# One fixed group for a unit's scores, another's sums and a third's transposes beside the first layer, and fewer pieces of w_out times phi

## The chip, the cores and the metric

The kernel runs on one NeuronCore of one Trainium2 chip. The metric is device time in microseconds (us): the median of several executions, beside one execution that the hardware profiler recorded.

## What is computed

The reference is a windowed attention followed by two mixture layers, in float32:

```python
# q, k, v: 4 batches x 8 heads x 576 positions x 64
scores = q @ k.T / 8                      # masked: a window of 32, or 32 dilated by 4
attn   = softmax(scores); x = attn @ v    # x becomes 2304 x 512
gate = sigmoid(x @ w_gate); val = x @ w_val      # 512 -> 1536
x    = (gate * val) @ w_out                      # 1536 -> 512
logits = x @ phi                                 # 32 slots
d = softmax over tokens(logits); slot_input = d.T @ x
slot_out = relu(slot_input @ w1[e]) @ w2[e]      # 8 experts, 4 slots each
out = softmax over slots(logits) @ slot_out
```

The kernel never forms x after `w_out`: it multiplies `w_out` by `phi` once (the tile `wp`) and takes the logits from the gated hidden values.

## The kernel before

**Token blocks and units.** Tokens are five blocks `n` (0 to 3 of 512 tokens, 4 of 256). A unit is one block and one pair of heads `hp`. Block 0's four units run at the start; the 16 units of blocks 1 to 4 are numbered z = 0 to 15 and run beside the first mixture layer. A unit has scores on PE (`scores`: one mask matmul and 32 small products, for each of two PSUM banks of the pool `ps_a`), a softmax on DVE, ACT and POOL (`softmax`, into `u["s"]`), four PE transposes (`turn_unit`, through a bank of `ps_m`, copied by ACT into a slot of `pt_ring`), the sums with v on PE (`weighted`, into the second halves of the score banks of a later unit, or for the last units into two banks of `ps_m`) and the copies into x, split into a high and a low part (`finish_unit`).

**The first layer.** `l1(n, f, ...)` computes feature block f (12 of them) of token block n: two halves (gate and value) of 12 matmuls of 512 columns into a bank of `ps_l1`. After each half it calls `between()`. Layer calls for block 0 and then block 1 give 48 such calls. A `Spread` object holds the list of unit steps and runs as many at a call as its marks make due. From the beginning of layer 0 on, the matmuls of the units go through `at()`, which pins an instruction behind everything traced before it on its engine; the layer's own matmuls and, before the change, the pieces of `w_out` times `phi` are not pinned, and the planner may place them earlier or later.

**The list of steps.** Unit z's scores, the sums of unit z - 2 and its copies are one step (`sp_step`), the transposes of unit z - 1 are another (`t_step`): 34 steps, 10 of them due by call 22, all by call 44.

**Weights.** `convert` takes staged 64-bit words (`st`, tag "l2", two buffers, 1 MB each) and makes float32 (`fw`), on ACT, DVE and POOL; the result is stored to DRAM at the next conversion. Conversions 12 to 17 are the six pieces of `w_out`, made during block 1's layer, one after each of its feature blocks 0 to 5; their `fw` use the tags "gb" and "xt" by turns ("xt" has one buffer). After each, `slot_weights` schedules four pieces for PE, each on a tick (a call of `between` during block 1): two of four transposes (`turned`), `product` and `summed`, beginning three ticks later.

**SP's queue.** All loads and stores up to the end of this layer are issued by SP in the order of the program: qk and v loads of units, staging loads, stores of converted weights, reloads of weights. The softmax of a unit of block 4 lives in the unused columns of its own qk buffer (two buffers), that of the other units in `sm4` (tag "x4").

After the first layer of blocks 0 and 1 come their logits and gathers (`Post`), blocks 2 and 3 as pairs (`pair_l1`), block 4, and the experts.

Of the kernel before, what the change touches and what calls it, by code (L numbers as in the profile page):

```python
# [7 lines left out]
F32 = mybir.dt.float32  # L8
# [9 lines left out]
P = 128  # L18
# [3 lines left out]
HP_ORDER = [0, 2, 1, 3]  # L22
NF = 12
# [6 lines left out]
SPL = (False, False)  # L30
NRM = True
C0 = 21
C1 = 19
WP = 1
ND = 4
# [21 lines left out]
def tile_kernel(  # L57
# [10 lines left out]
    nc = tc.nc  # L68

    cpool = ctx.enter_context(tc.tile_pool(name="cpool", bufs=1))  # L70
# [4 lines left out]
    ps_a = ctx.enter_context(tc.tile_pool(name="ps_a", bufs=4, space=PSUM))  # L75
# [1 line left out]

    BUFS = {
        "xa": 2, "xb": 2, "ga": 3, "gb": 3, "w": 2, "l2": 2,
        "qk": 2, "v": 2, "bd": 1, "xt": 1, "ws": 2, "x4": 1,  # L80
    }

    def b8(tag, shape, dt, name):
        return big.tile(shape, dt, tag=tag, name=name, bufs=BUFS[tag])
# [4 lines left out]
    ident = cst[:, 0 : C_I4 - C_ID]  # L89
    ones32 = cst[:, C_I4 - C_ID : C_PHI - C_ID]  # L90
    i4 = ones32[:, 0:32]
    phi = cst[:, C_PHI - C_ID : C_COLS - C_ID].rearrange("p (k s) -> p k s", k=ND)
    acc = cpool.tile([P, 3, 512], F32, name="acc")
# [43 lines left out]
    def at(ins):  # L137
        return tc.keep_in_program_order(ins) if grouped[0] else ins
# [52 lines left out]
    def turn_unit(u):  # L191
        s = u["s"].rearrange("p (c x) -> p c x", c=4)
        tr = ps_m.tile([P, 4, P], F32, tag="m", name="tr")
        for c in range(4):
            at(nc.tensor.transpose(tr[:, c], s[:, c], ident))  # L195
        nc.scalar.copy(pt_ring[:, u["z"] % 4].rearrange("p c i q -> p c (i q)"), tr)
# [53 lines left out]
            nc.scalar.copy(hi, xp[y])  # L250
            nc.vector.tensor_tensor(lo, xp[y], hi.bitcast(F32), ALU.subtract)  # L251

    sm4 = b8("x4", [P, 4, 512], F32, "sm4")
    early = [True]

    def ld(ins):
# [2 lines left out]
    def attn_steps(pbs, norm, head=None):  # L259
        jobs = [(n, hp) for n in pbs for hp in HP_ORDER]  # L260
        us = [{"id": j, "z": z} for z, j in enumerate(jobs)]
        tags = ["qk", "qk", "gb", "gb"] if head else ["qk"] * len(jobs)

        def load_qk(z):
            n, hp = jobs[z]
            w = 512 + k_cols(n, hp)
            us[z]["qk"] = b8(tags[z], [P, 2048], F32, "qk")
            us[z]["s"] = sm4[:, HP_ORDER.index(hp)] if n < 4 else us[z]["qk"][:, 1536:2048]
            ld(nc.sync.dma_start(us[z]["qk"][:, 0:w], qkv[n * NHP + hp, :, VCOLS : VCOLS + w]))

        def load_v(z):
            n, hp = jobs[z]
            if z % 2 == 0:
                v2 = b8("v", [P, 2, VCOLS], F32, "v2")
                us[z]["v"], us[z + 1]["v"] = v2[:, 0], v2[:, 1]
            ld(nc.sync.dma_start(us[z]["v"], qkv[n * NHP + hp, :, 0:VCOLS]))

        def load(z, what):
            if z < len(us) and not head:
                what(z)  # L280

        begun = []

        def first(what):
            if what not in begun:
                begun.append(what)
                what(0)
                what(1)

        def s_step(z, ts=range(4)):  # L290
            if z == 0 and 0 in ts:
                if head:
                    load_qk(0)
                    ld(nc.sync.dma_start(msk, masks.bitcast(BF16)))
                    load_qk(1)
                    ld(nc.sync.dma_start(cst, consts))
                    load_v(0)
                    load_qk(2)
                    load_v(1)
                    head()  # L300
                    load_qk(3)
                    load_v(2)
                    load_v(3)
                else:
                    first(load_qk)
                    first(load_v)
            scores(us[z], ts)
            if 3 not in ts:
                return
            if 2 <= z and not head:  # L310
                weighted(us[z - 2], range(2), us[z])
            softmax(us[z], norm)
            load(z + 2, load_qk)
            if z == 0:
                load(2, load_v)

        def t_step(z):
            turn_unit(us[z])

        def p_step(z, ts=range(2)):  # L320
            if head or z + 2 >= len(us):
                weighted(us[z], ts)
            if head:
                keep_warm(WP)
            if 1 in ts:
                finish_unit(us[z])
                load(z + 3, load_v)

        def sp_step(z):
            if z < len(jobs):  # L330
                s_step(z)
            if z >= 2:
                p_step(z - 2)

        steps = []
        for z in range(len(jobs) + (1 if head else 2)):
            turned = [(t_step, z - 1)] if 0 < z <= len(jobs) else []
            if head:
                score = [(s_step, z, [t]) for t in range(4)] if z < len(jobs) else []
                steps += score + turned + ([(p_step, z - 1, [t]) for t in range(2)] if z else [])  # L340
            else:
                steps += [(sp_step, z)] + turned
        return steps, lambda: first(load_qk), lambda: first(load_v)


# [21 lines left out]
    def convert(z):  # L367
        i = n_conv[0]
        n_conv[0] += 1
        stage(z)  # L370
        if i + 1 < len(turn):
            stage(turn[i + 1])
        st = staged[z]
        store()
        fw = b8(("ws", "ws", "gb", "xt")[i % 4] if i < NF else ("gb", "xt")[i % 2], [P, 2, 1024], F32, "fw")
        for h in range(2):
            c = slice(512 * h, 512 * h + 512)
            top, low = fw[:, 0, c], fw[:, 1, c]
            nc.scalar.activation(top, st[:, c, 1].bitcast(F32), AF.Prelu, scale=2.0**-112, alpha=2.0**32)  # L379
            nc.vector.tensor_scalar(top.bitcast(U32), top.bitcast(U32), 3, None, ALU.logical_shift_left)  # L380
            nc.vector.tensor_scalar(low.bitcast(I32), st[:, c, 0], 2.0**-29, None, ALU.mult)  # L381
            nc.gpsimd.tensor_tensor(low.bitcast(I32), top.bitcast(I32), low.bitcast(I32), ALU.add)  # L382
        if z < NF:
            stores.append((wg32[z // 2][:, z % 2], fw[:, 1]))
        else:
            y = z - NF
            stores.append((wo32[y // 2][:, 2 * (y % 2) : 2 * (y % 2) + 2].rearrange("p a c -> p (a c)"), fw[:, 1]))
            slot_weights(2 * y, fw[:, 1].rearrange("p (c x) -> p c x", c=2), 3)
        return fw[:, 1]

    ticks = [0]
    later = []
# [7 lines left out]
    def slot_weights(f, wo_f, lag):  # L400

        wt = pm.rearrange("p a b -> p (a b)").rearrange("p (k c x) -> p k c x", k=ND, c=2)
        at_ = {}

        def turned(c):
            wt_ps = ps_a.tile([P, ND, P], F32, tag="a", name="wt_ps")
            for kc in range(ND):
                nc.tensor.transpose(wt_ps[:, kc], wo_f[:, c, P * kc : P * kc + P], ident)
            nc.scalar.copy(wt[:, :, c], wt_ps)

        def product():
            pt_ps = ps_m.tile([P, 2, P], F32, tag="m", name="pt_ps")
            for kc in range(ND):
                nc.tensor.matmul(
                    pt_ps[32 * kc : 32 * kc + 32], lhsT=phi[:, kc, :], rhs=wt[:, kc], start=True, stop=True
                )
            at_["pt"] = cpool.tile([P, 2, P], F32, tag="pt", name="pt")
            nc.vector.tensor_copy(at_["pt"], pt_ps)

        def summed():  # L420
            wp_ps = ps_m.tile([P, 2, 32], F32, tag="m", name="wp_ps")
            for c in range(2):
                nc.tensor.matmul(wp_ps[:, c], lhsT=at_["pt"][:, c], rhs=i4, start=True, stop=True)
            nc.vector.tensor_scalar(wp[:, f : f + 2], wp_ps, 0.5, None, ALU.mult)

        for n, (step, *args) in enumerate(((turned, 0), (turned, 1), (product,), (summed,))):
            later.append((ticks[0] + lag + n, step, args))

    def split_w(src, pool=(True, False)):
        whl = b8("w", [P, 2, 2, ND, P], F32R, "whl")  # L430
# [454 lines left out]
    for z, (fn, *args) in enumerate(attn_steps([0], nc.vector, lambda: stage(0))[0]):  # L885
        fn(*args)
        if z == C0:
            steps, first_qk, first_v = attn_steps([1, 2, 3, 4], nc.gpsimd)
            sab = Spread(steps, [(2 * NF - 2, 10), (4 * NF - 4, len(steps))])
            ahead(0)  # L890
            first_qk()
            ahead(1)
            first_v()
# [128 lines left out]
    for f in range(NF):  # L1022
        c = f % 4
# [18 lines left out]
    for e in range(8):  # L1042
        for h in range(2):
            for kc in range(ND):
                nc.tensor.matmul(  # L1045
                    h_ps[h][32 * kc : 32 * kc + 32],
                    lhsT=st[:, kc, 32 * e : 32 * e + 32],
                    rhs=ew[0, e, h][:, kc],
# [230 lines left out]
```

## Time and profile before

| what | value |
|---|---|
| median of three runs | 498.02 us (497.69 to 499.08) |
| the profiled execution | 496.94 us |
| its span, first to last instruction | 495.2 us |
| PE busy | 468.6 us (95%) |
| DVE / ACT / POOL busy | 311.0 / 213.1 / 156.8 us |
| mean granted TensorE clock | 0.992 of full |

PE is TensorE's matmuls, PEld its weight loads, DVE VectorE, ACT ScalarE, POOL GpSimd, SP SyncE (here it only issues DMA). An `L` with a number is the line of the kernel that issued the instruction. The span is one execution; the median comes from others and also holds what lies around the span.

### The profile page before, as it was taken

Reading aid. Unit: us, or ns where it says so; the run is one execution under the profiler, and the core shown is the slowest. Engines: PE = TensorE matmul, PEld = TensorE weight load, DVE = VectorE, ACT = ScalarE, POOL = GpSimd, SP = SyncE. Lnnn points to the kernel's source line nnn. Section 1 sums busy time; section 2 is a strip of 40 time slices with the busy share of each in tenths; the row PEclk is TensorE's granted clock in tenths of the full one; section 3 lists DMA queues with packets and bytes.
Section 4 is the critical chain, followed back from the end, with each engine's and each line's share of the span. In section 5 each row is a group of like instructions: output and inputs, shape, how many; then the busy total and the mean of one; then the engine's idle time right before and its main releaser. Section 6 shows DMA issues by size and latency. Waiting matters only on the chain.

```text
span 495.2 us, 12830 instructions
## 1 busy us (share of the span) xinstructions
PE 468.6 (95%) x5488; PEld 357.3 (72%) x5488; DVE 311.0 (63%) x629; ACT 213.1 (43%) x414; POOL 156.8 (32%) x132
## 2 busy tenths in 40 slices
PE   6889999999899998999889999999999999999993
PEld 3558888887788876886557888888887889742552
DVE  3879898758666745436987656655547765541532
ACT  2455645435445534314744554554535343300223
POOL 0244536416445314235154323334212124110100
PEclk9899999999999999999999999999999999999998
DMA  8979978995896079120002201201499886579997
GB/s 301 421 276 361 351 234 306 310 344 195 322 368 253 2 253 394 63 86 1 1 1 86 85 25 61 86 5 80 142 372 422 345 326 259 190 296 367 428 402 239
DMA packets 23785, 112.14 MB, mean 226 GB/s; under 512 B 2352, under 2 KB 7216, under 8 KB 14640
## 3 DMA queue, kind: packets, MB, share of 16 engines
q1 hardware_dynamic: 23408, 111.06, 60.0%
q8 instruction: 43, 0.70, 0.6%
q10 hardware_dynamic: 320, 0.26, 0.2%
q14 instruction: 14, 0.11, 0.1%
HBM read 97.16 MB, written 14.16 MB: 225 GB/s over the span
## 4 chain that ended last, share of the span: by engine, by line
PE 80%; DVE 8%; DMA 4%; ACT 2%; issue 2%; POOL 1%; SPq 1%; DVEq 0%; ACTq 0%
PE l1ps L470 32%; PE pa L592 11%; PE pe L592 6%; PE tp L757 3%; PE s_ps L222 3%; PE h_ps L1045 3%; PE lt_ps L721 3%; PE pd L592 3%; PE s_ps L162 3%; PE so_ps L1104 3%; DMA wo<-fw 2%; PE sp L786 2%; PE tr L195 2%; DMA qk<-qkv 2%; DVE s L556 1%
## 5 line engine op out<-in xcount | busy, mean ns | idle before, releaser
L470 PE MATMUL l1ps<-x_hi,whl 128*128 128x512 f32 x384 | 129.4, 402 | 2.6 <-ACT x_hi L250 2.5
L470 PEld LDWEIGHTS l1ps<-x_hi,whl 128*128 128x128 f32 x384 | 71.7, 188 | 19.0 <-ACT x_hi L250 3.2
L470 PE MATMUL l1ps<-x_lo,whl 128*128 128x512 f32 x192 | 75.6, 394 | 0.0
L382 POOL TENSOR_TENSOR fw<-fw 128x512 int32<-128x512 int32 x36 | 49.0, 1370 | 61.7 <-DVE fw L381 24.7
L470 PEld LDWEIGHTS l1ps<-x_lo,whl 128*128 128x128 f32 x192 | 36.2, 188 | 6.6 <-DVE x_lo L251 0.2
L456 DVE SCALAR_TENSOR_TENSOR g<-g,l1ps 128x512 f32<-128x512 f32 (+1 forms) x36 | 21.4, 594 | 29.3 <-PE l1ps L470 29.0
L470 PE MATMUL l1ps<-x,whl 128*128 128x256 f32 x288 | 37.0, 285 | 0.0
L470 PEld LDWEIGHTS l1ps<-x,whl 128*128 128x128 f32 x288 | 35.4, 192 | 0.4 <-issue 0.2
L480 ACT ACTIVATE g<-l1ps 128x512 f32<-128x512 f32 (+1 forms) x36 | 18.9, 526 | 37.4 <-PE l1ps L470 37.4
L434 POOL TENSOR_TENSOR whl<-w,whl 128x512 fp32r<-128x512 f32 x12 | 15.9, 1326 | 51.2 <-ACT whl L433 39.7
L379 ACT ACTIVATE fw<-st 128x512 f32<-128x512 f32 x36 | 22.8, 675 | 12.4 <-DMA st<-wd 9.2
L757 PE MATMUL tp<-cst,g 128*128 128x128 f32 x216 | 28.0, 275 | 0.0
L757 PEld LDWEIGHTS tp<-cst,g 128*128 128x128 f32 x216 | 24.0, 140 | 5.0 <-issue 3.3
L762 ACT COPY gt<-tp 128x512 f32<-128x512 f32 x27 | 15.6, 584 | 25.0 <-PE tp L757 21.9
L176 DVE TENSOR_REDUCE mx<-s_ps 128x4 f32<-128x256 f32 x40 | 15.2, 413 | 14.3 <-PE s_ps L162 8.4
L380 DVE TENSOR_SCALAR fw<-fw 128x512 uint32<-128x512 uint32 x36 | 22.7, 640 | 1.9 <-ACT fw L379 1.0
L655 DVE TENSOR_TENSOR tm<-pe,tm 128x512 f32<-128x512 f32 x12 | 8.3, 691 | 24.1 <-PE pe L592 24.1
L434 DVE TENSOR_TENSOR whl<-fw,whl 128x512 fp32r<-128x512 f32 x24 | 20.9, 884 | 3.7 <-ACT whl L433 3.2
L381 DVE TENSOR_SCALAR fw<-st 128x512 int32<-128x512 uint32 x36 | 17.8, 528 | 7.7 <-DMA wst<-wg 3.7
L189 POOL TENSOR_TENSOR sm<-sm,su 128x512 f32<-128x512 f32 x12 | 13.6, 1130 | 28.3 <-DVE su L188 26.4
L434 POOL TENSOR_TENSOR whl<-wst,whl 128x512 fp32r<-128x512 f32 x12 | 15.9, 1326 | 19.0 <-ACT whl L433 11.7
L433 ACT CAST whl<-fw 128x512 fp32r<-128x512 f32 x24 | 14.6, 620 | 16.1 <-POOL fw L382 11.7
(455 smaller groups left out, 962.1 us busy)
## 6 DMA issues: line engine op xcount, KB each, us to landing
ew<-w SPq DMA_DIRECT2D x32, 1024.0 KB, 7.8
st<-wd SPq DMA_DIRECT2D x18, 1024.0 KB, 9.1
wst<-wg SPq DMA_DIRECT2D x12, 1024.0 KB, 7.7
v<-qkv SPq DMA_DIRECT2D x20, 512.0 KB, 6.1
wg<-fw SPq DMA_DIRECT2D x12, 512.0 KB, 7.8
w<-wg SPq DMA_DIRECT2D x6, 1024.0 KB, 7.5
qk<-qkv SPq DMA_DIRECT2D x10, 576.0 KB, 5.7
qk<-qkv SPq DMA_DIRECT2D x8, 528.0 KB, 5.5
```

The source lines that it names most:

```text
L176: nc.vector.tensor_reduce(mx[:, 4 * r : 4 * r + 4], u["s_ps"][r], AX.X, ALU.max)
L379: nc.scalar.activation(top, st[:, c, 1].bitcast(F32), AF.Prelu, scale=2.0**-112, alpha=2.0**32)
L380: nc.vector.tensor_scalar(top.bitcast(U32), top.bitcast(U32), 3, None, ALU.logical_shift_left)
L381: nc.vector.tensor_scalar(low.bitcast(I32), st[:, c, 0], 2.0**-29, None, ALU.mult)
L382: nc.gpsimd.tensor_tensor(low.bitcast(I32), top.bitcast(I32), low.bitcast(I32), ALU.add)
L434: (nc.gpsimd if pool[h] else nc.vector).tensor_tensor(whl[:, 1, h], src[:, h], whl[:, 0, h].bitcast(F32), ALU.subtract)
L456: return nc.vector.scalar_tensor_tensor(g, g, 1.0, val, ALU.add, ALU.mult)
L470: nc.tensor.matmul(pt[:, 0:nt], lhsT=whl[:, w_, a, dc, :], rhs=x_[n][:, dc, :], start=first, stop=(dc == HP_ORDER[-1] and w_ == 1),)
L480: nc.scalar.activation(g, pt[:, 0:nt], AF.Tanh, scale=0.5)
L592: nc.tensor.matmul(pt, lhsT=w[:, w_, P * c : P * c + P], rhs=x_[:, c], start=first and c == 0 and w_ == 0 and x_ is hi, stop=c == 1 and w_ ...
L757: nc.tensor.transpose(tp[:, c], g_sb[self.n, 4 * q + c][:, P * j : P * j + P], ident)
L762: nc.scalar.copy(to, tp)
```

## The change

Each group now holds, in program order: the scores of unit z, the sums of unit z - 3, the transposes of unit z - 2, the softmax of z, the loads, and the copies of unit z - 3. There are 19 steps, 7 due by call 22 and all by call 44. The softmax of block 4 gets a tile of tag "l2"; "xt" gets a second buffer. The pieces of `w_out` are three (both sets of transposes in one), pinned, and begin four ticks after a conversion, so that pieces of neighbouring conversions fall on the same ticks. The tile `pt` becomes a part of `acc`, and the descriptor scratch at the bottom of SBUF is set to 1024 bytes.

```diff
-        "qk": 2, "v": 2, "bd": 1, "xt": 1, "ws": 2, "x4": 1,
+        "qk": 2, "v": 2, "bd": 1, "xt": 2, "ws": 2, "x4": 1,
...
-            us[z]["s"] = sm4[:, HP_ORDER.index(hp)] if n < 4 else us[z]["qk"][:, 1536:2048]
+            if (n, hp) == (4, HP_ORDER[0]):
+                homes.append(b8("l2", [P, 4, 512], F32, "sm4"))
+            us[z]["s"] = homes[-1][:, HP_ORDER.index(hp)]
...
-            if 2 <= z and not head:
-                weighted(us[z - 2], range(2), us[z])
+            if 3 <= z and not head:
+                weighted(us[z - 3], range(2), us[z])
+                turn_unit(us[z - 2])
             softmax(us[z], norm)
...
-            if head or z + 2 >= len(us):
+            if head or z + 3 >= len(us):
                 weighted(us[z], ts)
...
-        def sp_step(z):
+        def group(z):
             if z < len(jobs):
                 s_step(z)
-            if z >= 2:
-                p_step(z - 2)
+            if z == 2 or len(jobs) <= z < len(jobs) + 2:
+                turn_unit(us[z - 2])
+            if z >= 3:
+                p_step(z - 3)
...
-        for z in range(len(jobs) + (1 if head else 2)):
+        for z in range(len(jobs) + (1 if head else 3)):
...
-                steps += [(sp_step, z)] + turned
+                steps.append((group, z))
...
-            slot_weights(2 * y, fw[:, 1].rearrange("p (c x) -> p c x", c=2), 3)
+            slot_weights(2 * y, fw[:, 1].rearrange("p (c x) -> p c x", c=2), LAG)
...
-        def turned(c):
+        def turned():
+            for c in range(2):
...
-            at_["pt"] = cpool.tile([P, 2, P], F32, tag="pt", name="pt")
+            at_["pt"] = acc[:, 2, 0:256].rearrange("p (c x) -> p c x", c=2)
...
-        for n, (step, *args) in enumerate(((turned, 0), (turned, 1), (product,), (summed,))):
-            later.append((ticks[0] + lag + n, step, args))
+        for n, step in enumerate((turned, product, summed)):
+            later.append((ticks[0] + lag + n, step, []))
...
-            sab = Spread(steps, [(2 * NF - 2, 10), (4 * NF - 4, len(steps))])
+            sab = Spread(steps, [(2 * NF - 2, 7), (4 * NF - 4, len(steps))])
...
-    nc = bacc.Bacc("TRN2", target_bir_lowering=False, num_devices=1)
+    nc = bacc.Bacc("TRN2", target_bir_lowering=False, num_devices=1, dynamic_dma_scratch_size=1024)
```

In the diff `LAG` is 4, and the transposes and products inside `turned`, `product` and `summed` are wrapped in `at()`.

## Rows read from the trace of the kernel before

**Rows 1.** The page: busy time, chain by engine, DMA issues with median landing.
```profile
PE 468.6 (95%) x5488; PEld 357.3 (72%) x5488; DVE 311.0 (63%) x629; ACT 213.1 (43%) x414; POOL 156.8 (32%) x132
...
PE 80%; DVE 8%; DMA 4%; ACT 2%; issue 2%; POOL 1%; SPq 1%; DVEq 0%; ACTq 0%
...
st<-wd SPq DMA_DIRECT2D x18, 1024.0 KB, 9.1
```
**Rows 2.** Stretches: us, busy and count by engine, clock, DMA share, GB/s.
```profile
40.00:80.00 40.00, 40.00 (x451) 32.70 (x443) 37.24 (x70) 21.50 (x40) 20.51 (x16) 1.00 0.90 314
```
**Rows 3.** Timeline of PE, 45 to 69 us: start, us, instruction, count.
```profile
46.21 0.48 PE L470 MATMUL l1ps<-x_hi,whl 128*128 128x512 f32 x1
...
51.79 0.39 PE L148 MATMUL s_ps<-msk 128*128 128x256 bf16 x2
52.11 0.86 PE L162 MATMUL s_ps<-qk 64*32 64x64 f32 x64
52.90 1.14 PE L222 MATMUL s_ps<-pt_ring,v 64*64 64x32 f32 x64
53.96 0.50 PE L470 MATMUL l1ps<-x_hi,whl 128*128 128x512 f32 x1
...
59.58 0.60 PE L195 MATMUL tr<-cst,sm 128*128 128x128 f32 x4
59.94 0.48 PE L470 MATMUL l1ps<-x_hi,whl 128*128 128x512 f32 x1
...
68.23 0.39 PE L148 MATMUL s_ps<-msk 128*128 128x256 bf16 x2
```
**Rows 4.** Timeline of PE, 189 to 194 us; in brackets idle before.
```profile
189.01 0.66 PE L408 MATMUL wt_ps<-cst,fw 128*128 128x128 f32 x4 [1.38 <-POOL fw L382]
...
191.42 0.48 PE L470 MATMUL l1ps<-x_hi,whl 128*128 128x512 f32 x1
...
193.18 0.86 PE L162 MATMUL s_ps<-qk 64*32 64x64 f32 x64
```
**Rows 5.** Timeline of SP, 154 to 178 us.
```profile
154.43 0.33 SPq L276 DMA_DIRECT2D v<-qkv  x1
175.37 0.33 SPq L269 DMA_DIRECT2D qk<-qkv  x1
...
176.59 0.43 SPq L361 DMA_DIRECT2D st<-wd  x1
177.06 0.43 SPq L365 DMA_DIRECT2D wo<-fw  x1
```
**Rows 6.** Chain of waits, 177 to 189 us: start, us, what.
```profile
177.06 8.92 DMA wo<-fw
...
187.59 1.38 POOL fw L382
```
**Rows 7.** Timeline of PE, 204 to 213 us.
```profile
204.71 0.60 PE L195 MATMUL tr<-cst,qk 128*128 128x128 f32 x4
...
209.06 0.50 PE L470 MATMUL l1ps<-x_hi,whl 128*128 128x512 f32 x1
...
212.01 1.19 PE L721 MATMUL lt_ps<-g,wp 128*32 128x128 f32 x36
```
**Rows 8.** Timeline of ACT at 205 us.
```profile
205.40 0.58 ACT L196 COPY pt_ring<-tr 128x512 f32<-128x512 f32 x1
```
**Rows 9.** Timeline of DVE at 210 us.
```profile
210.65 0.47 DVE L251 TENSOR_TENSOR x<-xp,x 128x128 fp32r<-128x128 f32 x2
```
**Rows 10.** The page's DMA queues: packets, MB, share.
```profile
q8 instruction: 43, 0.70, 0.6%
```
**Rows 11.** Chain of waits at 125 us.
```profile
125.27 1.29 issue
```
**Rows 12.** Stretches from the start to two stops: columns as in group 2.
```profile
0.00:22.86 22.86, 17.10 (x478) 10.07 (x478) 13.61 (x37) 7.16 (x12) 2.87 (x6) 0.93 0.94 357
0.00:125.06 125.06, 115.99 (x2007) 89.35 (x2007) 96.58 (x199) 59.78 (x112) 49.08 (x41) 0.99 0.86 311
```

More of the change, by code (lines that the diff above doesn't have):

```diff
@@ L32 @@
 C0 = 21
+LAG = 4
 C1 = 19
@@ L251, in finish_unit @@
             nc.vector.tensor_tensor(lo, xp[y], hi.bitcast(F32), ALU.subtract)
-    sm4 = b8("x4", [P, 4, 512], F32, "sm4")
+    homes = [b8("x4", [P, 4, 512], F32, "sm4")]
     early = [True]
@@ L327, in p_step @@
                 load(z + 3, load_v)
-        def sp_step(z):
+        def group(z):
             if z < len(jobs):
                 s_step(z)
-            if z >= 2:
-                p_step(z - 2)
+            if z == 2 or len(jobs) <= z < len(jobs) + 2:
+                turn_unit(us[z - 2])
+            if z >= 3:
+                p_step(z - 3)
         steps = []
-        for z in range(len(jobs) + (1 if head else 2)):
-            turned = [(t_step, z - 1)] if 0 < z <= len(jobs) else []
+        for z in range(len(jobs) + (1 if head else 3)):
             if head:
                 score = [(s_step, z, [t]) for t in range(4)] if z < len(jobs) else []
+                turned = [(t_step, z - 1)] if 0 < z <= len(jobs) else []
                 steps += score + turned + ([(p_step, z - 1, [t]) for t in range(2)] if z else [])
             else:
-                steps += [(sp_step, z)] + turned
+                steps.append((group, z))
         return steps, lambda: first(load_qk), lambda: first(load_v)
@@ L403, in slot_weights @@
         at_ = {}
-        def turned(c):
[L406 to L409, printed above, removed]
+        def turned():
+            for c in range(2):
+                wt_ps = ps_a.tile([P, ND, P], F32, tag="a", name="wt_ps")
+                for kc in range(ND):
+                    at(nc.tensor.transpose(wt_ps[:, kc], wo_f[:, c, P * kc : P * kc + P], ident))
+                nc.scalar.copy(wt[:, :, c], wt_ps)
         def product():
@@ L413, in product @@
             for kc in range(ND):
-                nc.tensor.matmul(
-                    pt_ps[32 * kc : 32 * kc + 32], lhsT=phi[:, kc, :], rhs=wt[:, kc], start=True, stop=True
+                at(
+                    nc.tensor.matmul(
+                        pt_ps[32 * kc : 32 * kc + 32], lhsT=phi[:, kc, :], rhs=wt[:, kc], start=True, stop=True
+                    )
                 )
-            at_["pt"] = cpool.tile([P, 2, P], F32, tag="pt", name="pt")
+            at_["pt"] = acc[:, 2, 0:256].rearrange("p (c x) -> p c x", c=2)
             nc.vector.tensor_copy(at_["pt"], pt_ps)
@@ L422, in summed @@
             for c in range(2):
-                nc.tensor.matmul(wp_ps[:, c], lhsT=at_["pt"][:, c], rhs=i4, start=True, stop=True)
+                at(nc.tensor.matmul(wp_ps[:, c], lhsT=at_["pt"][:, c], rhs=i4, start=True, stop=True))
             nc.vector.tensor_scalar(wp[:, f : f + 2], wp_ps, 0.5, None, ALU.mult)
-        for n, (step, *args) in enumerate(((turned, 0), (turned, 1), (product,), (summed,))):
-            later.append((ticks[0] + lag + n, step, args))
+        for n, step in enumerate((turned, product, summed)):
+            later.append((ticks[0] + lag + n, step, []))
     def split_w(src, pool=(True, False)):
```

## The prediction

> **What bounds the kernel now.** I read the chain of waits first, to know which engine sets the end, then busy time by stretches, then the timeline of PE in the stretch that the change touches, and last what PE waited for there. PE carries 80% of the chain [rows 1]. From 40 to 80 us it is busy 40.00 of 40.00 us, with ACT and POOL near half of that, DVE at 37.24 and the granted clock full [rows 2]. So beside the first layer (two token blocks, about 30 to 226 us) the time is the sum of what stands in PE's queue, plus its few waits. What another engine does counts only where it makes PE wait.
>
> **What a detour costs.** PE leaves the layer's matmuls for a unit's pieces and comes back. The run from 46.21 to 51.79 us is 24 matmuls in 5.58 us, the one from 59.94 to 68.23 is 36 in 8.29 us [rows 3]. The 12 more cost 2.71 us, 0.226 us each; so 24 would cost 5.42 us, and entering a run anew costs about 0.16 us; between runs of 24 and of 12 the same sum gives 0.13. I take 0.14 us a return. A detour of transposes is 0.36 us (59.58 to 59.94), one of mask, scores and weighted sums 2.17 us (51.79 to 53.96) [rows 3].
>
> **Returns saved.** In the timeline I counted 33 entries into runs of the layer's matmuls, from 46.21 [rows 3] to 209.06 us [rows 7]. Number the calls of the spread list 1 to 48, two to a feature block and 24 to a layer. The new list has 7 steps by call 22 and 19 by call 44, so step z runs at the first call whose due exceeds z: calls 1, 4, 7, 10, 13, 16, 19, 23, 24, 26, 28, 30, 32, 34, 35, 37, 39, 41, 43. Pieces of w_out, four ticks after a conversion and then on two ticks more, run at calls 30 to 42. From call 4 on that is 24 different calls, so 24 entries. Two places will not stay whole. Groups 16 and 17 turn a unit into one of the two banks of ps_m, sum another unit into two more, and are followed by a product that wants one again. The bank of the turn comes free after the ACT copy: turn at 204.71 [rows 7], copy from 205.40 for 0.58 us [rows 8], 1.27 us, of which the transposes hide 0.36. The banks of the sums come free after DVE: sums done at 209.06 [rows 7], the subtractions from 210.65 for 0.47 us [rows 9], so 2.06 us at most. The layer's matmuls are not pinned and can fill such waits: at 191.42 five of them stand inside a unit's work, before its scores at 193.18 [rows 4]. I count two cuts a group, four in all: 28 entries, 5 fewer than now, 5 x 0.14 = 0.70 us. Ends: 9 x 0.16 = 1.4 if nothing is cut, 0 if joining costs inside the group what it saves at its edge.
>
> The Trainium skill (TensorEngine Tiling (Array Packing), Tiling Modes, Key Properties) says that a change of tiling mode drains the engine. The transposes and the layer's matmuls both show 128*128, scores and sums 64*32 and 64*64 [rows 3]; the number of mode changes for a unit stays what it was, and by that rule joining them would give 0 instead of 0.70. The rows show the return behind transposes (the runs from 46.21 and 59.94) at nearly the cost of that behind sums (from 53.96 to 59.58, 24 matmuls in 5.62 us, 0.20 for the return) [rows 3], so I keep them.
>
> **The wait that goes.** SP issues in program order. After the v load at 154.43 us it issues nothing until 175.37: a qk load, whose buffer still holds the softmax of a unit of block 4 until its transposes [rows 5]. Behind it stand the staging of the last w_out piece (176.59) and the store of an earlier one (177.06) [rows 5]. That store takes 8.92 us and frees the only "xt" buffer; conversion starts then, the first half of POOL's last step ends at 187.59 + 1.38 = 188.97 us [rows 6], and the transposes on PE, begun at 189.01, had waited 1.38 us [rows 4]. The next feature block's weights are late behind it: the five matmuls from 191.42 take 1.76 us instead of 5 x 0.226 + 0.14 = 1.27 [rows 4], 0.49 more. The change takes away both causes: softmax of block 4 lives in an "l2" tile, so its qk buffer is free after the scores, and "xt" has two buffers. Gain 1.38 + 0.49 = 1.87 us; ends 2.0 and 0.
>
> What is late next: the new home takes one of the two staging buffers from softmax 12 (call 32, some 147 us) on. Staging 16 waits for conversion 15 (about 153), 17 for conversion 16 (about 164). A load takes 9.1 us at the median [rows 1], a conversion about 4.4 (186.0 to 188.97 and one more POOL step of 1.38 [rows 6]). The last is ready near 164 + 9.1 + 4.4 = 178 us; its transposes are pinned at call 40, which I put at 188 by adding up runs and groups. Ten microseconds of cover: I cost it at nothing. Without cover it costs what it costs now, 1.87 us.
>
> **Work only moved.** Scores, sums, transposes, products, qk and v loads are the same in number. ACT, DVE and POOL get a unit's work in larger lumps, and a softmax has two groups (three calls or more, over 9 us) until its transposes. ps_a holds two banks of scores and two of w_out transposes at calls 30, 32 and 34; at call 35 the next scores need the latter back, with a run of 2.7 us between. Nothing, at worst 1 us. What replaces the tile "pt" and the smaller descriptor scratch only make room: 0.
>
> **Code loading.** PE stops for 1.29 us at 125.27 us inside a unit's sums, with "issue" and no semaphore as the cause [rows 11]. The instruction queue moved 43 packets in 0.70 MB [rows 10], 16 KB each, for 2 x 5,488 matmuls and weight loads [rows 1]: 255 each. Such stops stand where PE has run 956 and 4,014 of them (both counts of a row added) [rows 12]; the difference, 3,058, is twelve blocks of 256 less the queue's own waits, which aren't counted. So a block was not there when PE reached its edge. In the layer a block lasts 128 x 0.226 = 29 us; inside a group (66 + 64 + 4 matmuls with their weight loads, 268 instructions in 2.17 + 0.36 = 2.5 us) one lasts 2.4. A group longer than a block, with an edge near its start, runs into the next edge before the fetch is done. Counting on from 956 by the new order, edges fall within some 30 instructions of the start at groups 4, 7, 11 and 14, the last two with 284 instructions in a row. The joined group lasts 0.36 us longer, so a hit costs 1.29 - 0.36 = 0.9 us; as I know the edges only to a few instructions, I take 0.5 for each: 2.0 against 1.29 now, a loss of 0.7. Ends: gain 1.3 (no edge hits) and loss 2.3 (four of 0.9).
>
> **Sum.** 1.87 + 0.70 - 0.70 = 1.87 us. The profiled execution took 496.94 us, 495.2 of it span and 1.7 around it; it would become 495.1. The median of the runs shown, 498.02, lies 1.1 above that execution, so 498.02 - 1.87 = **496.2 us**. By the chain PE leads behind the layer too, so I let the gain pass to the end in full.
>
> **The rivals.** A measurement tells about 0.3% (1.5 us) from no change.
> (a) Forecast: wait gone, some returns saved, code stops a bit costlier: 494.9 to 497.2. Chance 0.48, of which 0.34 is faster by over 0.3% and 0.14 within it.
> (b) Clean: edges miss the groups, no cut: 498.0 - 1.9 - 1.4 - 1.3 = 493.4, to 494.9. For it: the edges depend on a few instructions that I can't count. Chance 0.20, faster.
> (c) It doesn't do what it says: the groups stay cut, or code stops reach 2.3 us of loss, and only the wait at 189 goes: 498.0 - 1.9 + 0 to 2.3 = 496.1 to 498.4, say 497.3. That layer matmuls float into pinned work [rows 4] speaks for it. The Trainium skill's rule on modes gives 498.0 - 1.87 + 0.7 = 496.8 and falls here. Chance 0.18: 0.16 within 0.3%, 0.02 faster.
> (d) Slower: the banks of ps_m at groups 16 and 17. If the layer's matmuls don't fill, PE waits 0.91 us for the turn's copy and 2.06 for the sums, twice: 5.9 us, and with the rest of the sum (less 0.56 for the cuts then not made) 498.0 - 1.9 - 0.6 + 5.9 = 501.4. It decides once over half of it is unfilled. Against it: 191.42 again. Chance 0.14, 0.13 of it slower and 0.01 within.
>
> Together: faster 0.56, within 0.3% 0.31, slower 0.13. The range runs from the clean case to where the slower one begins, 493.0 to 498.9; some 0.02 lie below it, most of (d) above, and a little for what I haven't seen.
>
> **What the next profile would show.** SP has no hole of 20 us near 155 to 175; the transposes of the last w_out piece don't wait for POOL; 25 to 30 runs of the layer's matmuls; each unit as mask, scores, sums, transposes in a row; "issue" stops of PE at groups 4, 7, 11 or 14, within a block of each other's edge. The logits of block 0 start near 210 us instead of 212.01 [rows 7]. Wrong would be: waits of xp or pt_ps on ACT or DVE copies over 1 us, wt_ps waiting for POOL again, or an earlier logits start that the stretch behind, where DVE is dense, gives back.

## The result and the profile after

The changed kernel takes 500.36 us (median of 20 runs, 498.33 to 503.31) against 497.95 for the kernel before in the same rounds: a ratio of 1.0051, 95% interval 1.0034 to 1.0067. The forecast was 496.2 in 493.0 to 498.9, so it is wrong in sign and outside its range. The profiled execution took 501.15 us with a span of 499.4.

The page of the changed kernel answers to [rows 1] with hardly a difference in busy time: PE is busy 2.0 us longer, and loads land sooner. The chain's shares are smaller (PE 58% for 80%) because here it can be followed back no further than 159.79 us, to the last of the waits below.

```profile
PE 470.6 (94%) x5483; PEld 358.3 (72%) x5488; DVE 312.9 (63%) x629; ACT 214.7 (43%) x414; POOL 158.8 (32%) x132
...
PE 58%; DVE 6%; ACT 1%; issue 1%; POOL 0%; DVEq 0%; ACTq 0%
...
st<-wd SPq DMA_DIRECT2D x18, 1024.0 KB, 8.3
```

Where the time went is read from four stretches with the same work in both: the head, the first layer with the groups (from the first mask matmul beside it to the first `lt_ps`), from there to the first `si_ps`, and the end. First the kernel after, then the kernel before; columns as in [rows 2].

```profile
0.00:34.94 34.94, 25.86 (x642) 17.24 (x645) 24.21 (x57) 14.57 (x27) 7.64 (x10) 0.90 0.91 351
34.94:214.85 179.91, 175.06 (x2720) 139.06 (x2719) 126.43 (x262) 86.04 (x164) 76.87 (x59) 1.00 0.74 259
214.85:441.95 227.10, 221.10 (x1627) 178.93 (x1630) 143.76 (x271) 103.08 (x201) 70.58 (x59) 1.00 0.39 148
441.95:499.40 57.45, 48.58 (x502) 23.07 (x502) 18.52 (x39) 11.06 (x22) 3.74 (x5) 0.95 0.88 342
```

```profile
0.00:34.73 34.73, 25.66 (x644) 16.13 (x645) 23.19 (x57) 14.24 (x27) 7.65 (x10) 0.95 0.93 354
34.73:212.01 177.28, 174.47 (x2719) 139.40 (x2719) 125.84 (x262) 84.71 (x164) 74.95 (x59) 1.00 0.73 263
212.01:439.00 226.99, 221.09 (x1629) 178.93 (x1632) 143.47 (x271) 103.07 (x201) 70.45 (x59) 1.00 0.39 148
439.00:495.20 56.20, 47.39 (x502) 22.88 (x502) 18.52 (x39) 11.06 (x22) 3.74 (x5) 0.96 0.90 351
```

The layer is 2.63 us longer, and the next stretch hands this on unchanged (227.10 and 226.99). The layer's 2.63, in one execution of each kernel, is about the difference of the medians (2.41). The end adds 1.25 in this one execution; it is taken up under the hardware below. Inside the layer, PE is busy 0.59 us more and stands idle 4.85 us instead of 2.81, that is 2.04 more. The list of what PE waited for names all four idle times of the layer over 0.1 us (us in total, times, longest):

```profile
PE l1ps L479 <- ACT g L489: 2.1, 2, 1.1
PE wt_ps L415 <- issue: 1.9, 1, 1.9
...
PE pt_ps L422 <- ACT pm L416: 0.9, 1, 0.9
```

Before there were 1.29 of "issue" [rows 11], 1.38 for `fw` [rows 4] and 0.15 for `whl`. So the wait that was to go went, the code stop (idle time of PE before which the trace shows no releaser, listed as "issue") stayed, and three waits for ACT are new.

**The tanh waits.** In PE's timeline of the changed kernel group 3 stands whole, as mask, scores, sums and transposes, and the run of 36 layer matmuls behind it takes 9.61 us (64.02 to 73.63) for the 8.29 of [rows 3]:

```profile
61.43 0.39 PE L149 MATMUL s_ps<-msk 128*128 128x256 bf16 x2
...
63.60 0.66 PE L196 MATMUL tr<-cst,sm 128*128 128x128 f32 x4
64.02 0.48 PE L479 MATMUL l1ps<-x_hi,whl 128*128 128x512 f32 x1
...
69.33 0.39 PE L479 MATMUL l1ps<-x_hi,whl 128*128 128x512 f32 x1
70.77 0.50 PE L479 MATMUL l1ps<-x_hi,whl 128*128 128x512 f32 x1 [1.05 <-ACT g L489]
...
73.63 0.39 PE L149 MATMUL s_ps<-msk 128*128 128x256 bf16 x2
```

ACT's timeline of the same kernel there:

```profile
66.07 0.62 ACT L442 CAST whl<-fw 128x512 fp32r<-128x512 f32 x1 [0.64 <-POOL fw L388]
66.59 0.58 ACT L197 COPY pt_ring<-tr 128x512 f32<-128x512 f32 x1
67.07 0.67 ACT L385 ACTIVATE fw<-st 128x512 f32<-128x512 f32 x1
68.44 0.37 ACT L251 CAST x_hi<-s_ps 128x256 fp32r<-128x256 f32 x1 [0.70 <-DVE sm L179]
68.78 0.63 ACT L185 ACTIVATE sm<-sm 128x512 f32<-128x512 f32 x1
69.31 0.36 ACT L251 CAST x_hi<-s_ps 128x256 fp32r<-128x256 f32 x1
69.56 0.67 ACT L385 ACTIVATE fw<-st 128x512 f32<-128x512 f32 x1
70.13 0.59 ACT L489 ACTIVATE g<-l1ps 128x512 f32<-128x512 f32 x1
```

Groups 3 and 5 run at calls 10 and 16. The tanh is the activation of the gate (`g<-l1ps` on ACT). An even call follows a value half, so the next half is a gate half, and its tanh must empty one of the two banks of `ps_l1` before the half after next. The gate half of group 3 was done at about 66.8 us (64.02 and twelve matmuls), but ACT first did the ring copy (`pt_ring`), both x copies, the exp (on `sm`) and two steps of weight conversion (`fw`), with a wait of 0.70 for DVE among them; the tanh began at 70.13. The same happens at 93.83, behind group 5 (1.01). Groups 4, 6 and 7, at odd calls of the same layer, before a value half, have no such wait. But neither have group 1 (call 4) and groups 8 to 13 (calls 24 to 34), all at even calls: an even call alone does not make the tanh late. That the weight conversions beside groups 3 and 5 are the other half of it is argued from the timeline above, and no run tests it by itself.

**The code stop and the pm wait,** in PE's timeline: at group 11 the queue stood still between the unit's transposes and the joined transposes of w_out; at 159.84 the product waited for the copy of the second half, which ACT did only at 159.22, behind an x copy that had itself waited 1.90 us for the softmax on DVE.

```profile
142.38 0.66 PE L196 MATMUL tr<-cst,sm 128*128 128x128 f32 x4
144.95 1.03 PE L415 MATMUL wt_ps<-cst,fw 128*128 128x128 f32 x8 [1.91 <-issue]
...
159.84 0.64 PE L422 MATMUL pt_ps<-pm,cst 128*32 128x256 f32 x8 [0.88 <-ACT pm L416]
```

### The profile page after: what moved, and what is told of

Same layout as the page of the kernel before. It is cut to its first block, busy times and chain, and to the rows that moved or that the text cites. A ratio compares the mean times of both kernels' runs of the same rounds, so it can differ in the third digit from the quotient of the medians.

```text
span 499.4 us, 12798 instructions
## 1 busy us (share of the span) xinstructions
PE 470.6 (94%) x5483; PEld 358.3 (72%) x5488; DVE 312.9 (63%) x629; ACT 214.7 (43%) x414; POOL 158.8 (32%) x132
## 4 chain that ended last, share of the span: by engine, by line
PE 58%; DVE 6%; ACT 1%; issue 1%; POOL 0%; DVEq 0%; ACTq 0%
PE l1ps L479 16%; PE pa L601 11%; PE pe L601 6%; PE tp L766 3%; PE so_ps L1113 3%; PE h_ps L1054 3%; PE lt_ps L730 3%; PE pd L601 3%; PE sp L795 2%; PE op L1152 1%; DVE s L565 1%; DVE t_hl L506 1%; PE si_ps L1033 1%; PE wt_ps L415 1%; DVE gt L769 1%
## 5 line engine op out<-in xcount | busy, mean ns | idle before, releaser
L388 POOL TENSOR_TENSOR fw<-fw 128x512 int32<-128x512 int32 x36 | 50.8, 1420 | 60.5 <-DVE fw L387 26.9
L443 DVE TENSOR_TENSOR whl<-fw,whl 128x512 fp32r<-128x512 f32 x24 | 23.6, 992 | 6.5 <-ACT whl L442 5.9
L190 POOL TENSOR_TENSOR sm<-sm,su 128x512 f32<-128x512 f32 x16 | 17.7, 1103 | 30.8 <-DVE su L189 24.4
L442 ACT CAST whl<-wst 128x512 fp32r<-128x512 f32 x24 | 13.8, 616 | 23.6 <-issue 10.1
L387 DVE TENSOR_SCALAR fw<-st 128x512 int32<-128x512 uint32 x36 | 19.9, 580 | 2.0 <-DMA st<-wd 2.0
```

What stands on the lines that cost most here:

```text
L190: norm.tensor_tensor(s, s, su.unsqueeze(2).to_broadcast([P, 8, 64]), ALU.mult)
L442: nc.scalar.copy(whl[:, 0, h], src[:, h])
L443: (nc.gpsimd if pool[h] else nc.vector).tensor_tensor(whl[:, 1, h], src[:, h], whl[:, 0, h].bitcast(F32), ALU.subtract)
```

## The experiments

All times are medians; the kernel before took 498.2, 498.3, 498.1 and 497.8 us in the four series. "Layer" is the second stretch above, "idle" the sum of PE's idle times over 0.1 us in it; both come from one profiled execution, the ratio from all. The intervals of the single cures e2_odd, e5_pad and e6_fin overlap with that of the changed kernel, so what each of them gains is read from that one execution; the intervals of e3_supply, e9_three, e13_pieces and e14_groups_cured lie below it.

| kernel | layer | idle | median | ratio to before, interval |
|---|---|---|---|---|
| before | 177.28 | 2.81 | 497.95 | |
| after | 179.91 | 4.85 | 500.36 | 1.0051 [1.0034, 1.0067] |
| e1_edges | 179.01 | 3.36 | 502.63 | 1.0103 [1.0069, 1.0137] |
| e2_odd | 178.63 | 3.83 | 499.39 | 1.0038 [1.0013, 1.0063] |
| e3_supply | 177.51 | 3.25 | 498.01 | 0.999 [0.997, 1.001] |
| e4_free | 179.72 | 3.72 | 499.43 | 1.0033 [1.0008, 1.0058] |
| e5_pad | 179.46 | 4.27 | 500.57 | 1.0039 [1.0016, 1.0062] |
| e6_fin | 178.50 | 3.01 | 499.35 | 1.0023 [1.0005, 1.0041] |
| e7_both | 179.31 | 3.65 | 501.16 | 1.0061 [1.0038, 1.0085] |
| e8_turn | 179.76 | 2.98 | 500.54 | 1.0046 [1.0022, 1.007] |
| e9_three | 177.15 | 1.87 | 497.44 | 0.9999 [0.9974, 1.0025] |
| e10_odd_pad | 177.36 | 2.08 | 499.01 | 1.002 [0.9995, 1.0044] |
| e11_xt1 | 180.03 | 4.46 | 499.82 | 1.0039 [1.0012, 1.0065] |
| e12_before_pad | 179.32 | 3.50 | 499.68 | 1.0043 [1.0011, 1.0075] |
| e13_pieces | 178.13 | 3.54 | 497.85 | 0.9992 [0.9969, 1.0015] |
| e14_groups_cured | 176.44 | 1.58 | 497.65 | 0.9996 [0.9966, 1.0025] |

**e1_edges: other block edges.** 25 more warming matmuls at the start, so that every later instruction of PE's queue stands 50 places further.

```diff
-SMALL = 70
+SMALL = 95
```

> The changed kernel with 25 more of the tiny matmuls that fill PE's wait for the first load: 50 more instructions ahead of everything, so that no group of 268 or more instructions begins within some 25 instructions of a block edge. Theory 1 (the 1.91 us stop in the transposes of group 11 is a code block that was not there in time): that stop goes, the first logits start about 2 us earlier than 214.85 us, the time falls from 500.4 to about 498.4 us. Rival (the stop belongs to that place, a transfer or a semaphore not shown): it stays at group 11, time as after.

No "issue" stop is left in the layer, so the stop at group 11 belongs to its place in the queue. But the head got a new one, and the tanh waits gave way to 0.34, 0.55 and, for DVE's product, 1.09, with 1.38 for pm. The groups stand at the same calls as in the changed kernel, so the call does not decide on the tanh waits alone. Of the whole time this kernel tells little: the layer begins at 40.09 us, 5 later. What PE waited for longest in this kernel:

```profile
PE s_ps L163 <- issue: 3.5, 1, 3.5
```

**e2_odd: groups 1, 3 and 5 one call later** (calls 5, 11 and 17), given as a list.

```diff
-sab = Spread(steps, [(2 * NF - 2, 7), (4 * NF - 4, len(steps))])
+sab = Listed(steps, [1, 5, 7, 11, 13, 17, 19, 23, 24, 26, 28, 30, 32, 34, 35, 37, 39, 41, 43])
```

> The changed kernel with the groups of layer 0 at calls 1, 5, 7, 11, 13, 17, 19, 23, 24 instead of 1, 4, 7, 10, 13, 16, 19, 23, 24; the rest at the same calls. Theory 1 (the two waits of PE for ACT's tanh, 1.05 and 1.01 us, come from where groups 3 and 5 fall against the conversions and the split of weights): both go, about 2.6 us less, 497.8 us. Rival (a joined group is too much for ACT and DVE wherever it stands): such waits show behind the moved groups, 500.4 us.

Both tanh waits are gone, as a wait of their place should. In their place stand a second code stop (1.25 at group 4, 1.11 at group 11) and 0.58 for DVE; the pm wait stays (0.90). The layer gains 1.28 of the 2.06.

**e3_supply: the kernel before with only what was to take the wait at 189 us away** (second "xt" buffer, the "l2" home, and the room for them).

```diff
-"xt": 1
+"xt": 2
...
+if (n, hp) == (4, HP_ORDER[0]):
+    homes.append(b8("l2", [P, 4, 512], F32, "sm4"))
```

> The kernel before with only the second xt buffer, the l2 home for the softmax of block 4, the piece of acc for pt and the smaller scratch; steps and pieces as before. Theory 1 (SP's hole cost 1.9 us at 189 us and no more): hole and wait go, 1.9 us faster than before, about 496.1 us. Rival (the hole was hidden, or the home starves the staging): same as before, 498.0 us, with a wait of the transposes for POOL at another place.

The wait goes, the code stop shrinks to 0.39, and still the layer doesn't get shorter (177.51): pieces come earlier and wait for DVE, 1.00 at 149.9, 1.39 at 178.2 and 0.46 at 204.6. Nor does the run. Two of these in the list of this kernel's waits:

```profile
PE pt_ps L416 <- DVE wp L426: 1.4, 1, 1.4
...
PE wp_ps L425 <- DVE acc L420: 1.0, 1, 1.0
```

**e4_free: the groups without the joined pieces** (four to a conversion, not pinned, three ticks behind it).

```diff
-LAG = 4
+LAG = 3
...
-for n, step in enumerate((turned, product, summed)):
+for n, (step, *args) in enumerate(((turned, 0), (turned, 1), (product,), (summed,))):
```

> The changed kernel with the pieces of w_out as before: four a conversion, not pinned, from three ticks on. Theory 1: the wait of a product for ACT's copy (0.88 us at 159 us) goes, the block edges of the later groups move; 499.4 us, or 497.5 if the code stop happens to go too. Rival (the joined pieces are where the loss is): all of the 2.4 us come back, 498.0 or less.

Both tanh waits are there (1.04 and 1.16, with 0.28 for DVE between them), the pm wait isn't, and there are code stops of 0.49 and 0.76. The groups alone carry the loss of the layer (179.72).

**e5_pad: 23 tiny matmuls behind the head's last unit,** 46 instructions of shift with no work in the layer.

```diff
+if z == 3 and 1 in ts:
+    for i in range(23):
+        kept(nc.tensor.matmul(idle[g, 0:32], lhsT=zero[:, 0:32], rhs=zero[:, 512:544], start=True, stop=True))
```

> The changed kernel with 23 tiny matmuls pinned behind the last sums of block 0's units, where PE waits 0.75 us for x anyway: 46 more instructions ahead of the layer and nothing moved in the head. Theory 1 (block edges): the stop of 1.9 us at group 11 goes, no code stop in the layer, from the first scores of the layer to the first logits 177.8 us instead of 179.9, time about 498.4 us. Rival (25 matmuls at the start cost 4 us because more instructions cost anywhere): as slow as that, over 502.

The stop at group 11 is gone (0.51 is left, at 37.0); tanh 1.05 and 1.01 as before, but pm now 1.70. Of 1.91 taken away the layer keeps 0.45.

**e6_fin: a unit's closing and its v load one call behind its group,** so that the x copies don't stand in the group's lump on ACT. The calls are given as a list, with the groups where they were.

```diff
-            if 1 in ts:
+            if head and 1 in ts:
                 finish_unit(us[z])
...
+                steps += [(finish, z - 3)] if z >= 3 else []
```

> The changed kernel with the copies of x (and the v load behind them) one call after the group. Theory 1 (ACT's copy of x shares a PSUM bank with the new scores, so it stands still until DVE has subtracted the maximum, and the tanh and the copy of the w_out transposes stand behind it): the waits of PE for tanh (2.06 us) and for that copy (0.88 us) go; layer stretch 176.7 us if the code stop stays, time 497.6. Rival (ACT and DVE are simply too full beside a conversion): the waits stay, 500.4.

The pm wait goes, the tanh waits stay (0.77 and 1.19): the x copies as such are not what makes the tanh late. 1.05 remains where the code stop was, put down to ACT; it stands at the same count of instructions as the code stops (see "Code loading" below), so it may be that stop under another name. The layer gains 1.41.

**e7_both: closing later, 30 tiny matmuls, and the product one tick later.**

```diff
-later.append((ticks[0] + lag + n, step, []))
+later.append((ticks[0] + lag + (0, 2, 3)[n], step, []))
```

> Copies of x one call later, 30 tiny matmuls for the block edges, and the products one tick later (transposes, then two ticks on the product, then the sum). Theory 1: hardly any wait left in the layer stretch, 175.3 us against 177.3 before, time 496.0 us, 2 us under the kernel before. Rival (waits move on, whatever one takes away): 498 or more.

A miss: tanh 0.77 and 1.17, and the later product leads to a wp_ps wait for DVE of 1.36.

**e8_turn: the transposes ahead of the scores in a group,** behind layer matmuls instead of behind sums.

```diff
+            if 3 <= z and not head:
+                turn_unit(us[z - 2])
             scores(us[z], ts)
...
-                turn_unit(us[z - 2])
```

> The changed kernel with a unit's transposes ahead of the next scores instead of behind the sums. Theory 1 (joining saves at the group's edge what the transposes lose behind the sums, 0.41 us instead of 0.35): the transposes take 0.35 to 0.43 us and the returns to the layer 0.16 instead of 0.12; nothing gained, 500.4 or up to 0.5 less. Rival (the order of tiling modes matters): 13 groups x 0.1 to 0.2 us less, 498.5.

Added up from start to next start less idle, the 64 transposes of the layer take 7.15 us, for 7.60 in the changed kernel and 6.80 before. The waits of the layer are 1.87 us less (0.46 for the tanh, 0.42 for DVE, no pm wait, 2.10 of code stop), yet the layer is only 0.15 shorter, because PE's own work is 1.72 more. That is the clock: from the end of the code stop on, 145.6 to 149.0 us, the granted clock was 0.50, the lower level of 1.2 GHz. Two microseconds of e8_turn, and then of the changed kernel:

```profile
146.00:148.00 2.00, 2.00 (x9) 1.90 (x9) 2.00 (x6) 1.04 (x2) 1.64 (x2) 0.50 0.94 359
146.00:148.00 2.00, 2.00 (x10) 1.62 (x10) 1.97 (x3) 1.44 (x4) 1.64 (x2) 1.00 1.05 368
```

The eight transposes of w_out and the twelve layer matmuls there took 5.51 us without the stop, and 3.72 in the changed kernel. That is 1.79 more, so the rest of PE's work in the layer is the same within 0.1 us: what the transposes save is given back elsewhere. Of the layer's own matmuls, which rise from 122.60 to 123.52, 0.85 of the 0.92 stand in that stretch.

**e9_three: the three cures at once** (e2's calls, e6's closing, e5's 23 tiny matmuls).

> The changed kernel with three cures at once: groups 1, 3 and 5 one call later, a unit's closing and its v load one call after its group, and 23 tiny matmuls behind the head. Theory A (the loss is the sum of the new waits of the first layer, each with a cause of its own): the two tanh waits (1.05 and 1.01 us), the pm wait (0.88) and the code stop at group 11 (1.91) all go, what is left of waits is under 1.5 us, the stretch is 176 to 177.3 us against 179.91, and the run comes to 496.5 to 498, no slower than the kernel before. Theory B (ACT and DVE have too little slack in the first layer, so that a wait that is taken away comes back at the next conversion): new waits for DVE's g or acc of 1 us and more, the stretch stays at 178.3 to 179 us, the run at 499 to 500.

Tanh, pm and the long code stop are gone; what is left is 0.53 and 0.54 of "issue", 0.59 and 0.21 for DVE. The layer is back to the length it had before, and so is the run. By stretches:

```profile
0.00:34.74 34.74, 26.04 (x668) 17.13 (x668) 24.16 (x57) 14.32 (x27) 7.63 (x10) 0.95 0.93 352
34.74:211.89 177.15, 175.23 (x2720) 139.31 (x2719) 127.47 (x262) 85.23 (x164) 77.48 (x59) 1.00 0.74 263
```

ACT's timeline in e9_three shows why the later call helps. At group 3 the tanh runs first, then the same lump, and the next tanh waits for PE and not PE for it:

```profile
66.14 0.59 ACT L497 ACTIVATE g<-l1ps 128x512 f32<-128x512 f32 x1
66.63 1.27 ACT L393 ACTIVATE fw<-st 128x512 f32<-128x512 f32 x2
68.19 0.59 ACT L197 COPY pt_ring<-tr 128x512 f32<-128x512 f32 x1 [0.29 <-PE tr L196]
69.39 0.37 ACT L251 CAST x_hi<-s_ps 128x256 fp32r<-128x256 f32 x1 [0.61 <-DVE sm L179]
...
73.65 0.60 ACT L497 ACTIVATE g<-l1ps 128x512 f32<-128x512 f32 x1 [0.88 <-PE l1ps L487]
```

The closing one call later is no part of what this spot shows: here too the x copy stands in the lump (69.39), of an earlier unit.

**e10_odd_pad: the same without the later closing.**

> Groups 1, 3 and 5 one call later and 23 tiny matmuls, the closing of a unit left in its group. Theory A: as the last kernel but with the pm wait of about 0.9 us near 159 us still there: stretch 177 to 178.2 us, 497.5 to 498.7. Theory B: 178.3 to 179 us, 499 to 500. Either way no code stop at groups 4 and 11, where the groups moved alone still had 1.25 and 1.11 us.

As theory A has it: no tanh waits, no code stop over 0.4, the pm wait at its place (0.89), and 0.56 and 0.24 for DVE as in e9_three. The layer is 177.36; the median lies 1.6 above e9_three, but the two intervals overlap.

**e11_xt1: the changed kernel with one "xt" buffer.**

```diff
-"xt": 2
+"xt": 1
```

> The changed kernel with one xt buffer for two. If the wait of 1.38 us at 189 went because of the second buffer: SP stands idle for 10 to 20 us about 155 to 175 us, a wt_ps or wp_ps wait of 1 to 2 us comes back behind 178 us, and the stretch grows from 179.9 to 181 to 182 us (501.5 to 502.5). If it went because the groups free the buffer earlier: no such hole, no such wait, time unchanged at 500.4.

No wait for POOL comes back, nor any behind 178 us: the layer is 180.03, and SP goes on issuing where it stood for 20 us [rows 5]. Where the code stop stood there is 1.06 now, put down to ACT, and two other code stops take 0.79 and 0.46; the pm wait is gone although the closing stayed in the group. SP's timeline in this kernel:

```profile
153.73 0.33 SPq L279 DMA_DIRECT2D v<-qkv  x1
158.18 0.33 SPq L367 DMA_DIRECT2D st<-wd  x1
158.60 0.38 SPq L371 DMA_DIRECT2D wo<-fw  x1
162.83 0.33 SPq L272 DMA_DIRECT2D qk<-qkv  x1
```

**e12_before_pad: the kernel before with 40 tiny matmuls behind the head.**

> The kernel before with 40 tiny matmuls behind the head (80 instructions on TensorE's queue). If the issue stop of 1.29 us at 125 us belongs to the place of a boundary of 256 instructions among the small matmuls: it goes, the stretch is 176 us against 177.28 plus some 0.1, and the run 496.5 to 497 against 498, unless the shift opens another stop, which then stands at another of the places where such a boundary falls among pieces. If it belongs to the group that runs there: it stays at 125 us with 1.3 us and the run at 498.

The stop at 125 us goes and one of 1.14 comes at 146.3, so it belongs to the edge and not to the group; but the wait for `fw` at 191.2 grows to 2.26, and the layer to 179.32. Only 0.69 of the 2.04 is idle time. The rest is the clock again: 1.4 us behind that wait, from 192.6 to 196.0 us, the granted clock was 0.50.

```profile
193.00:195.00 2.00, 2.00 (x11) 1.98 (x10) 1.49 (x3) 1.13 (x4) 1.88 (x2) 0.50 1.04 426
```

The work from the mask (192.62) to the scores (196.55) took 3.93 us, for 2.59 and 0.15 idle before: 1.34 more, which is all of the rest. Whether the clock falls so in its other executions (median 499.68) is not shown.

**e13_pieces: the joined pieces without the groups,** on the kernel of e3_supply.

> The kernel before with the buffers of the change and with its joined, pinned pieces (three for four, four ticks behind a conversion), but the units' scores and transposes as separate steps as before: the pieces without the groups. Theory A (the loss comes from where the groups fall against the conversions): no tanh waits of 1 us at 70 and 94, the wp_ps waits for DVE that the same buffers had with the old pieces (1.00 at 150, 1.39 at 178, 0.46 at 205) are smaller, stretch 176 to 177.5 us, 497 to 498. Rival (the pieces carry the loss): stretch over 178.5 us, 499 to 500.5, with wt_ps or pt_ps waits of 1 us and more between 140 and 200.

No tanh waits; a code stop of 0.97, and again pieces waiting for DVE (1.55, 0.55, 0.47). The layer, 178.13, is longer than theory A said; the run is that of the kernel before.

**e14_groups_cured: the three cures on the groups with the old pieces.**

> The three cures at once on the kernel with groups and with the pieces of before (four to a conversion, not pinned, three ticks behind): the groups without the joined pieces, cured. If joining the pieces is worth something by itself, this is slower than the 497.4 of the cured kernel with joined pieces, by what 5 or 6 returns of 0.14 and the unpinned pieces' waits give: 0.7 to 2 us, 498.1 to 499.5, stretch 177.8 to 179. If joining them gives back inside the group what it saves at its edge, as the transposes' sums of the changed kernel say (0.80 against 0.84): 497 to 497.8 and a stretch within 0.5 us of 177.15.

176.44 and 497.65: nothing is lost without the joined pieces. So each pair differs by the joined pieces: without groups e3_supply and e13_pieces (177.51 and 178.13), with groups e4_free and the changed kernel (179.72 and 179.91), with cured groups this kernel and e9_three (176.44 and 177.15). Joining the pieces gains nothing that these runs can tell, with or without the groups; the groups alone lose, and lose nothing once their waits are cured.

## Why the prediction was wrong, step by step

**The step that failed** is "Work only moved ... Nothing, at worst 1 us". It looked at when data would be ready for a group and not at what the group's lump on ACT holds up: the layer's own tanh, next in ACT's queue behind groups 3 and 5, and the copy `pm`. Measured: 1.05 + 1.01 + 0.88 = 2.94 us. e2_odd, e10_odd_pad and e9_three show that groups 3 and 5 one call later leave no tanh wait, and e9_three against e10_odd_pad, alike but for the closing, that a closing one call later takes the pm wait away. Neither is the only way: the tanh waits shrank in e1_edges and e8_turn with the groups at the same calls, and the pm wait is gone in e8_turn and e11_xt1 too. Why even the groups of e6_fin, without their own x copies, leave the tanh late is only argued: exp, conversions and DVE's wait remain in the lump.

**Returns saved** was put at 0.70, with 0 as its lower end, and came out below that. The cuts at groups 16 and 17 came as predicted, as after 190.50 in PE's timeline of the changed kernel; counted from the first group, 35 entries became 29.

```profile
189.96 0.60 PE L196 MATMUL tr<-cst,sm 128*128 128x128 f32 x4
190.50 0.29 PE L223 MATMUL xp<-pt_ring,v 64*64 64x16 f32 x2
190.71 0.50 PE L479 MATMUL l1ps<-x_hi,whl 128*128 128x512 f32 x1
...
195.96 1.07 PE L415 MATMUL wt_ps<-cst,fw 128*128 128x128 f32 x8
```

But the group from 61.43 to 64.02 takes 2.59 us, where the two detours of [rows 3] took 2.17 and 0.36. Summed as for e8_turn, transposes rose by 0.80 us and the layer's matmuls fell by only 0.22 (restarts behind the new waits are in it); mask, scores and sums rose by 0.16, `wt_ps` by 0.15, and `wp_ps` fell by 0.31. Together 0.58, which is PE's 0.59 more busy time. It stays so where the waits are cured: layer less idle is 0.81 above the kernel before in e9_three and 0.39 in e14_groups_cured. The rule that the prediction set against its rows, that a change of tiling mode drains the engine (the Trainium skill, TensorEngine Tiling (Array Packing), Tiling Modes, Key Properties), gives 0 for this term, and here the traces agree that nothing was to be saved: behind the sums the transposes took longer, and in e8_turn, where they stand elsewhere, PE's work without the stretch of low clock was the same.

**The wait that goes** went, as predicted: SP has no hole, and the last transposes at 195.96 above wait for nobody. Its two causes were not both needed: e11_xt1 shows that with the "l2" home one "xt" buffer is enough in the new order. But e3_supply shows that the gain of 1.87 was not to be had by this alone even in the old order.

**Code loading** was put at 0.70 of loss with edges at groups 4, 7, 11 and 14; it came as one stop at group 11, 1.91 for 1.29, a loss of 0.63. The place is one of the four, and e1_edges and e5_pad show the cause by moving it. That the sum agrees is partly luck: the picture was four hits of 0.5, and one edge cost all of it, more than the 0.9 that a hit was to cost at most. The blocks of 256 themselves hold: all 19 idle times of over 0.1 us of "issue" in the layers of the sixteen profiles begin where the matmuls, weight loads and other instructions that PE's queue has run (4,799 in the changed kernel, 4,034 before, for example) leave 191 to 194 when divided by 256. The 1.05 of e6_fin and the 1.06 of e11_xt1, put down to ACT, do so too (4,801 each).

**The sum.** Forecast -1.87, measured +2.63 in the layer, 4.50 apart: 2.94 from the moved work, 1.29 from the returns (-0.70 forecast, +0.59 found), 0.34 from the wait (1.87 forecast; 1.38 + 0.15 found), less 0.07 from the code stops. The slow rival (d) did not happen, since the layer's matmuls do fill the wait for the banks of `ps_m`; that its 501.4 lies near the measured time is luck, its mechanism was wrong.

## What to carry to other kernels

Before joining small steps into one group, write out each engine's queue behind the group and look at what the bottleneck engine wants next from it: a lump of over 3 us on an engine that is half idle (ACT 86 of 180 us busy) costs as much as it delays the one short instruction that frees a bank. Place groups by that instruction (here two groups one call later were enough), and compare a group's cost inside, between its own modes, before counting a saving at its edge. Where several engines are near the pace, judge an edit with its waits cured one by one and all at once: single cures gave 0.45 to 1.4 us of the layer, all three 2.8. And look at the granted clock of a stretch before putting a longer one down to the edit: in e8_turn it hid 1.7 us.

## What the runs showed of the hardware

A stop at a code edge is not of fixed size: 1.29 us in the kernel before, 1.91 in the changed one, 2.10 in e8_turn, 3.5 in the head of e1_edges. 46 to 80 instructions of padding far ahead take it away or bring it up at another place.

Four transposes of 128 columns take 0.42 us behind sums and until the layer's next matmul (63.60 to 64.02), and 0.36 between layer matmuls [rows 3].

The end stretch, from `si_ps` on, took 57.4 to 58.0 us in nine of the sixteen profiles and 56.2 to 56.5 in seven. In each of the nine, and in none of the seven, the granted clock is down in the first four microseconds of it. Stretches of 2 us about the beginning of `si_ps`, in the kernel after and in e9_three:

```profile
440.00:442.00 2.00, 1.78 (x16) 1.17 (x20) 0.56 (x1) 0.00 (x0) 0.00 (x0) 0.75 0.88 369
442.00:444.00 2.00, 2.00 (x12) 0.51 (x16) 0.00 (x0) 0.00 (x0) 0.00 (x0) 0.50 0.20 82
```

```profile
437.00:439.00 2.00, 1.78 (x16) 1.18 (x19) 0.56 (x1) 0.00 (x0) 0.00 (x0) 1.00 0.88 369
439.00:441.00 2.00, 2.00 (x24) 0.52 (x16) 0.00 (x0) 0.00 (x0) 0.00 (x0) 1.00 0.46 131
```

From 442 to 444 us the changed kernel has 0.50, the lower level of 1.2 GHz, and does half as many matmuls in these 2 us (12 for 24); `si_ps` takes 4.00 us there and 2.78 in e9_three. Before it PE did the same in both: `dg_ps` in 2.87 us, a little `busy`, a gap of 0.2. e13_pieces, with the units in the order of before, has the long end too, e9_three, e10_odd_pad and e11_xt1, with groups and joined pieces, the short one. The two falls in the layer, in e8_turn and e12_before_pad, came at the end of one idle time of PE and 1.4 us behind another, of 2.10 and 2.26 us, the two longest in the layers of these profiles. What makes the clock fall in one execution and not in another stays open. The clock does not explain the loss: over a whole execution the mean granted clock was below 0.989 in 7 of 20 executions of the changed kernel and in 30 of the 115 of the kernel before in the four series, and the medians of the others are 499.9 and 497.8 us. The fall at the end is 1.25 of the 4.2 us between the two profiled executions, and no part of the layer's 2.63.
